# Tokens' rows scattered straight to their expert's part of a buffer, read back by plain loads; token ids stored 256 bytes apart

## The chip, the cores and the metric

The kernel runs on one core of one Trainium2 chip. The metric is the time of one execution on the device in microseconds (us). Before the change three executions took 4009.82, 4017.08 and 4010.77, with a median of 4010.77.

## What is computed

Three layers follow each other: a spectral filter over the sequence, a mixture of 8 experts in which each token goes to one, and a dense layer with a squared relu.

```python
# x (8, 3072, 256); filt_r, filt_i (1537, 256); moe_w1 (8, 256, 1024), moe_w2 (8, 1024, 256)
X = np.fft.rfft(x, axis=1)
y = np.fft.irfft(X * (filt_r + 1j * filt_i)[None], n=3072, axis=1)      # 24576 tokens of 256
logits = y @ w_gate;  e_idx = argmax(logits);  gate_w = softmax(logits)[e_idx]
eom = 1 / (1 + exp(-(y @ w_output_gate)))
for e in range(8):                                                    # MoE1: only the tokens of e
    out[mask] = gate_w * eom[:, e] * (relu(y[mask] @ w1[e]) @ w2[e])
h = relu(out @ moe2_w_in);  result = h * h @ moe2_w_out                  # MoE2: 256 -> 2048 -> 256
```

## The kernel before

The filter is done as matrix products in stages. Stage a loads x, stage b does the second half of the transform, the multiplication by the filter (in part on GpSimd, L340) and the first half of the inverse, stage c the last half. The eight batches are taken as four groups of two, and a group of stage c gives six chunks `yo` of 128 x 8 tokens. A row of a chunk has 272 floats (1088 bytes): 256 values, then logits and the scale of the token. `route` finds each token's expert and its rank there, with a running count per expert in `carry`. Products are made of operands split into a high and a low part of reduced precision (tiles with names in h and l), so each product is three matmuls, and the split costs ScalarE and VectorE a pass each.

Routing before: a chunk is stored to `yd` in token order (L471, 24 stores of 1088 KB). The slot that a token has among its expert's tokens is computed, and `scatter` (L405) writes the row number of each token, 4 bytes, to that slot of a table in DRAM, 128 tokens per indirect DMA on GpSimd, 192 in all. There are four tables, taken in turn, which twelve stores of zeros clear at the start; a reader adds the four.

MoE1 takes tiles of tokens of one expert. The first four (`KP`), of the expert with most tokens in the first three groups, are worked while stage c is still busy with the last group: this is called the lead stage here. After the last group `tables` computes on VectorE which expert, slot and output column each of the other 58 tiles has (37 wide ones of 512 tokens, 21 narrow ones of 256, two wide and one narrow in turn). For a tile `start_t` reads these three numbers into SP's registers (L714) and loads the tile's piece of the four tables (L719), `list_rows` adds them on VectorE, and `gather` (L739) fetches the rows from `yd` by 128 per indirect DMA on GpSimd, at step f = 4 of the tile two ahead. `load_w` loads 512 KB of weights per quarter tile on SP (L727, L728). `scale_x` and `turn_x` scale and transpose the rows (L765, L777, L782), `up` and `down` are the two products (L798, L814) with eight steps f each. At its end a tile stores its result to `ytd` (L822) and the row numbers of its tokens to `idsc` (L823). For a narrow tile row c x 128 + p lies on partition p, so that every piece of that store is 4 bytes; for a wide tile partition p has four tokens in a row, and a piece is 16 bytes.

During MoE1 the weights of MoE2 are decoded from 64-bit floats: `decode` loads a raw piece on SP (L612, 32 pieces of 256 KB) and works it on VectorE (from L617) between MoE1's own work. MoE2 loads 512 tokens of `ytd` and their ids, and scatters its result to the output's rows on GpSimd (L937, 192 in all).

Each engine works its instructions in program order. The order of the work between stages is a list of steps written out beforehand; in a step the generators named above issue their next piece. SP holds most DMAs, so a DMA there comes behind all that SP was given before; SP's DMAs take eight semaphores in turn, so one waits for the landing of the eighth before it. Buffers from pools make a writer wait for the last reader of the same buffer.

Of the kernel before, what the change touches and what calls it, by code (L numbers as in the profile page):

```python
# [11 lines left out]
F32 = mybir.dt.float32  # L12
# [17 lines left out]
SEG = NT  # L30
TP = E * SEG // 128 + 16
TT = 512
TC = 8
TS = 256

# [65 lines left out]
def spectral_moe_kernel(ctx: ExitStack, tc: tile.TileContext, x, filt_r, filt_i, w_gate, w_og, w1, w2,  # L101
# [6 lines left out]
    yd = dram.tile([NT + 1, YW], F32, name="yd")  # L108

    NTAB = 4  # L110
    ytd = dram.tile([D, NT + TT], F32, name="ytd")
    idsc = dram.tile([NT + TT, 1], I32, name="idsc")
    tab = [dram.tile([128 * TP, 1], I32, name=f"tab{i}") for i in range(NTAB)]
    tabv = [t.rearrange("(p c) o -> p (c o)", p=128) for t in tab]

# [9 lines left out]
    nc.gpsimd.iota(rowid, pattern=[[2 * S, PR], [1, N2]], base=1, channel_multiplier=N2)  # L125
# [31 lines left out]
    const.tile([128, 72], F32, name="pad")  # L157
    pl = {"xsm": ctx.enter_context(tc.tile_pool(name="xsm", bufs=2, side="right"))}
    right = lambda stack, name, bufs, **kw: stack.enter_context(tc.tile_pool(name=name, bufs=bufs, side="right", **kw))
    pl["xsm"].tile([128, 24], F32, name="xpad", bufs=1)  # L160
# [7 lines left out]
    zi = fcon.tile([128, E * SEG // 384], I32, name="zi")  # L168
    nc.gpsimd.memset(zi, 0)
# [88 lines left out]
    nc.scalar.dma_start(out=yd[0:1], in_=zrow)  # L258
# [103 lines left out]
    ydv = yd[1:NT + 1].rearrange("(p q j) d -> q p (j d)", p=PR, j=N2)  # L362
# [38 lines left out]
    def scatter(n):  # L401

        for _ in range(min(n, len(scat))):
            si, a, g, n = scat.pop(0)
            nc.gpsimd.indirect_dma_start(  # L405
                out=tab[nscat[0] % NTAB], out_offset=bass.IndirectOffsetOnAxis(ap=si[:, a:a + 1], axis=0),
                in_=rowid[:, g, n:n + 1], in_offset=None)
            nscat[0] += 1

    def route(c):  # L410
# [52 lines left out]
        sn, sq = (rp.tile([128, TC], I32, name=n, bufs=1) for n in ("sn", "sq"))  # L463
        nc.vector.tensor_copy(sn, sl)
        nc.vector.tensor_scalar(sq, sn, 7, None, op0=ALU.logical_shift_right)
        nc.vector.tensor_scalar(sn, sn, 127, None, op0=ALU.bitwise_and)
        nc.vector.scalar_tensor_tensor(si, sn, float(TP), sq, op0=ALU.mult, op1=ALU.add)
        if ncarry[0] == GP * UC // 4:
            nc.vector.tensor_tensor(cnt_p, c1, segb, ALU.subtract)
        yield  # L470
        later.append(lambda: nc.sync.dma_start(out=ydv[:, g, 2 * j0 * YW:(2 * j0 + TC) * YW],  # L471
                                               in_=t.rearrange("p j w -> p (j w)")))
        for a in range(TC):
            scat.append((si, a, g, 2 * j0 + a))
# [58 lines left out]
    def find_lead():  # L533
# [12 lines left out]
        v.tensor_scalar(leadi[:, 1:2], leadi[:, 1:2], 7, None, op0=ALU.logical_shift_right)  # L546

    def tables():
# [49 lines left out]
        v.tensor_scalar(tabi[:, 1:2], tabi[:, 1:2], 7, None, op0=ALU.logical_shift_right)  # L598
# [100 lines left out]
    W, WR, X, cols, ereg = {}, {}, {}, {}, {}  # L699
# [12 lines left out]
    def start_t(t):  # L712
        w = width[t]
        e, s, cols[t] = (nc.sync.value_load(tabi[slot[t - KP]:slot[t - KP] + 1, i:i + 1], min_val=0, max_val=m)  # L714
                         for i, m in enumerate((E - 1, (E * SEG - w) // 128, NT)))
        n = w // 128
        ti = pl["xsm"].tile([128, NTAB * 4], I32, name="ti", bufs=4)
        for i in range(NTAB):
            nc.sync.dma_start(out=ti[:, i * n:(i + 1) * n], in_=tabv[i][:, ds(s, n)])  # L719
        X[t] = ti  # L720
        ereg[t] = e
# [9 lines left out]
    def gather(t):  # L731
        n = width[t] // 128
        if t < KP:
            idx = idx_p[0][:, t * n:(t + 1) * n]
        else:
            idx = list_rows(X[t], n)
        xg = pl["xgq"].tile([128, 4 * YW + 2 * E], F32, name="xg", bufs=1)
        for c in range(n):
# [29 lines left out]
    def turn_x(t, h):  # L768
        xs, idx = X[t][:2]
        if h == 0:  # L770
            X[t] = xs, idx, *(pl["xgp"].tile([128, 2, TT], F32R, name=n) for n in ("xh", "xl"))
# [366 lines left out]
```

## Time and profile before

| | us |
|---|---|
| median of three executions | 4010.77 |
| profiled execution | 4012.15 |
| its span, first to last instruction | 4010.2 |
| TensorE busy in the span | 3841.1 (96%) |
| VectorE, ScalarE, GpSimd busy | 2836.9, 2000.6, 775.8 |
| mean granted clock of TensorE (share of full speed) | 0.982 |

The span runs from the filter (to about 720, with the lead stage from about 625), over MoE1 (to about 1970) to MoE2. The profile names an instruction by line, engine and operation, with out<-in by the program's tile names. "Idle before" is how long the engine had nothing to run, with what ended it: an instruction, a DMA that landed, or "remote", a semaphore event that no instruction in the trace explains. "PEclk" is the granted clock of TensorE. "SPq" rows are DMAs issued by SP; they are not busy time. A share of DMA is the mean over the core's 16 DMA engines, and may pass 1 where transfers are counted in a window that they only touch.

### The profile page before, as it was taken

The numbers are of one execution on the slowest core, as the hardware profiler recorded it, in microseconds if no ns is written. First come the engines' busy times: TensorE is split into PE (matmuls) and PEld (weight loads), VectorE is DVE, ScalarE is ACT, GpSimd is POOL, SyncE is SP. The second block draws the span as 40 slices with busy tenths as digits, with TensorE's granted clock in tenths as the row PEclk, the third lists the DMA queues.
The fourth block names the chain that finished last, engine by engine and source line by source line (L and its number), as shares of the span: only waits on it lengthen the run. The fifth ranks groups of instructions, "written<-read, shape, count | busy, mean of one in ns | idle before, by whom it ended". The sixth has DMA issues, their size and how long they took to land.

```text
span 4010.2 us, 75055 instructions
## 1 busy us (share of the span) xinstructions
PE 3841.1 (96%) x27556; PEld 3573.5 (89%) x27556; DVE 2836.9 (71%) x5265; ACT 2000.6 (50%) x3957; POOL 775.8 (19%) x743
## 2 busy tenths in 40 slices
PE   8988897898999999999999999999999999999998
PEld 7777775687788888888899999999999999999998
DVE  7576675477788886666677777777777777777775
ACT  6364553244445445455455555555555555555554
POOL 3354545311111111211001011010110100101001
PEclk9999998999999999999999999999999999999999
DMA  6323222155666666666300000000000000000000
GB/s 222 105 78 114 89 75 72 59 151 145 154 155 175 172 161 164 158 159 162 100 22 28 28 25 30 22 28 28 24 28 26 27 28 23 27 27 26 29 17 17
DMA packets 270773, 318.74 MB, mean 79 GB/s; under 512 B 82082, under 2 KB 215427, under 8 KB 267331
## 3 DMA queue, kind: packets, MB, share of 16 engines
q1 hardware_dynamic: 244128, 259.71, 23.6%
q0 software_dynamic: 25248, 53.99, 4.5%
q8 instruction: 216, 3.54, 0.4%
q14 instruction: 155, 1.26, 0.1%
q10 hardware_dynamic: 1026, 0.23, 0.0%
HBM read 231.55 MB, written 82.26 MB: 78 GB/s over the span
## 4 chain that ended last, share of the span: by engine, by line
PE 87%; DVE 4%; DMA 3%; another core or an unknown queue 2%; issue 2%; ACT 1%; SPq 0%; POOL 0%; DVEq 0%; POOLq 0%; ACTq 0%
PE py L928 26%; PE ph L882 17%; PE ph L798 12%; PE py L814 12%; PE px L882 7%; PE o L357 3%; PE p L378 2%; PE o L392 2%; PE p L278 2%; PE p L331 1%; PE p L335 1%; PE p L306 1%; PE px L777 1%; DMA raw<-in_moe_w_in_dram 1%
## 5 line engine op out<-in xcount | busy, mean ns | idle before, releaser
L928 PE MATMUL py<-woh,hh 128*128 128x256 f32 x3072 | 857.1, 279 | 0.0
L928 PE MATMUL py<-woh,hl 128*128 128x256 f32 x3072 | 852.8, 278 | 0.4 <-DVE hl L915 0.4
L928 PE MATMUL py<-wol,hh 128*128 128x256 f32 x3072 | 852.9, 278 | 0.0
L928 PEld LDWEIGHTS py<-woh,hl 128*128 128x128 f32 x3072 | 579.8, 189 | 0.9 <-DVE hl L915 0.8
L928 PEld LDWEIGHTS py<-woh,hh 128*128 128x128 f32 x3072 | 579.9, 189 | 0.0
L928 PEld LDWEIGHTS py<-wol,hh 128*128 128x128 f32 x3072 | 576.3, 188 | 0.0
L937 POOL DMA_INDIRECT out_dram<-ou,io x192 | 207.9, 1083 | 1868.6 <-ACT C L904 1634.6
L802 ACT ACTIVATE hh<-ph 128x512 fp32r<-128x512 f32 (+1 forms) x496 | 261.2, 527 | 596.9 <-PE ph L798 537.8
L882 PE MATMUL ph<-bh,wsh 128*128 128x256 f32 x1920 | 542.1, 282 | 5.1 <-ACT s L889 2.7
L882 PE MATMUL ph<-bl,wsh 128*128 128x256 f32 x1920 | 537.6, 280 | 0.1
L882 PE MATMUL ph<-bh,wsl 128*128 128x256 f32 x1920 | 537.3, 280 | 0.0
L906 DVE SCALAR_TENSOR_TENSOR q<-C 128x1024 f32<-128x1024 f32 x384 | 470.2, 1224 | 1.9 <-ACT C L904 1.9
L915 DVE TENSOR_TENSOR hl<-q,hh 128x1024 fp32r<-128x1024 f32 x384 | 467.1, 1216 | 1.1 <-ACT hh L913 1.1
L803 DVE SCALAR_TENSOR_TENSOR hl<-ph,hh 128x512 fp32r<-128x512 f32 (+1 forms) x496 | 296.4, 598 | 232.5 <-ACT hh L802 205.8
L900 DVE TENSOR_TENSOR C<-ph,p 128x256 f32<-128x256 f32 x384 | 163.1, 425 | 399.7 <-ACT hh L913 397.4
L913 ACT CAST hh<-q 128x1024 fp32r<-128x1024 f32 x384 | 403.9, 1052 | 1.3 <-DVE q L906 1.3
L904 ACT COPY C<-ph 128x256 f32<-128x256 f32 x384 | 144.1, 375 | 501.2 <-PE ph L882 501.2
L739 POOL DMA_INDIRECT xg<-yd,idx x190 | 199.4, 1050 | 948.9 <-DVE idx L749 902.0
L882 PEld LDWEIGHTS ph<-bh,wsh 128*128 128x128 f32 x1920 | 362.4, 189 | 8.3 <-ACT s L889 4.1
L814 PE MATMUL py<-hh,wh 128*128 128x512 f32 (+1 forms) x992 | 363.4, 366 | 0.0
L882 PEld LDWEIGHTS ph<-bl,wsh 128*128 128x128 f32 x1920 | 360.8, 188 | 0.3 <-DVE bl L860 0.3
L882 PEld LDWEIGHTS ph<-bh,wsl 128*128 128x128 f32 x1920 | 360.9, 188 | 0.0
(267 smaller groups left out, 8772.1 us busy)
## 6 DMA issues: line engine op xcount, KB each, us to landing
r<-in_moe_w_dram SPq DMA_DIRECT2D x472, 256.0 KB
yd<-yo SPq DMA_DIRECT2D x24, 1088.0 KB
xt<-in_x_dram SPq DMA_DIRECT2D x48, 512.0 KB
r<-ytd SPq DMA_DIRECT2D x48, 512.0 KB
ytd<-yt SPq DMA_DIRECT2D x41, 512.0 KB
ytd<-yt SPq DMA_DIRECT2D x21, 256.0 KB
raw<-in_moe_w_in_dram SPq DMA_DIRECT2D x16, 256.0 KB
raw<-in_moe_w_out_dram SPq DMA_DIRECT2D x16, 256.0 KB
```

Source lines behind the costliest of these rows:

```text
L739: nc.gpsimd.indirect_dma_start(out=xg[:, c * YW:(c + 1) * YW], out_offset=None, in_=yd[0:(NT * GP // NG if t < KP else NT) + 1], in_offset ...
L798: nc.tensor.matmul(ps, a[:, c, f2 * 128:(f2 + 1) * 128], b[:, c, 0:w], start=n == 0, stop=n == 5)
L802: nc.scalar.activation(hh, ps, AF.Relu)
L803: nc.vector.scalar_tensor_tensor(hl, ps, 0.0, hh.bitcast(F32), op0=ALU.max, op1=ALU.subtract)
L814: nc.tensor.matmul(Y[t][h], a[:, f % 2, h * 128:(h + 1) * 128], b, start=f == 0 and i == 0, stop=f == NF - 1 and i == 2)
L882: nc.tensor.matmul(ps, x[:, u, a], y[:, b], start=start and n == 0, stop=n == 2, skip_group_check=True)
L900: nc.vector.tensor_tensor(C[:, 3], V, p5, ALU.add)
L906: nc.vector.scalar_tensor_tensor(q, C, 0.0, C, op0=ALU.max, op1=ALU.mult)
L913: nc.scalar.copy(hh, q)
L915: nc.vector.tensor_tensor(hl, q, hh.bitcast(F32), ALU.subtract)
L928: nc.tensor.matmul(Z[t][k][:, c, :], x[:, 2 * i + k, c * 128:(c + 1) * 128], w[:, 2 * u + i, :], start=u == 0 and m in (0, 6), stop=u == N ...
L937: nc.gpsimd.indirect_dma_start(out=out, out_offset=bass.IndirectOffsetOnAxis(ap=io[:, c:c + 1], axis=0), in_=ou[:, c, :], in_offset=None)
```

## The change

Routing after: each chunk's rows go straight from the chunk to their slots in one DRAM buffer `srt`, in which every expert has room for all tokens and 256 more (`SEG`), by the same 192 indirect DMAs (L404), now with 1088 bytes per token. GpSimd writes the row number into a spare column of the chunk beforehand (L464). `yd`, its stores, the four tables, their clearing and loads, and `list_rows` are gone. `gather` is one plain load per tile on SP (L731) at f = 3. Behind each expert's last row 256 rows of zeros are stored by `tables` (L598, L599), at addresses read from the counts. The ids come with the rows: `scale_x` copies them (L752) and `put_ids` stores them one step later (L738), each 4 bytes to a row of 256 bytes in `idsc`, in one layout for all tiles. The scatters of chunks and of the output, and the lead tiles' gathers, are declared not to overlap, so that they don't wait for each other. In MoE2 the last unit's matmuls (L926, in `down2`) close half 0 of the output at m = 11 instead of 17.

```diff
-SEG = NT
-TP = E * SEG // 128 + 16
+SEG = NT + TS
...
+    srt = dram.tile([E * SEG, YW], F32, name="srt")
+    srtv = dram_disjoint_views(srt, NG * N2 + E)
+    outv = dram_disjoint_views(out, NT // 128)
...
+    idsc = dram.tile([NT + TT, 64], I32, name="idsc")
+    def apart(i, others, own):
+
+        tc.declare_no_dep(i.ins, group=others, reason="other rows")
+        tc.add_to_no_dep_group(own, i.ins)
...
     def scatter(n):
 
         for _ in range(min(n, len(scat))):
-            si, a, g, n = scat.pop(0)
-            nc.gpsimd.indirect_dma_start(
-                out=tab[nscat[0] % NTAB], out_offset=bass.IndirectOffsetOnAxis(ap=si[:, a:a + 1], axis=0),
-                in_=rowid[:, g, n:n + 1], in_offset=None)
+            t, si, a = scat.pop(0)
+            i = nc.gpsimd.indirect_dma_start(
+                out=srtv[nscat[0]], out_offset=bass.IndirectOffsetOnAxis(ap=si[:, a:a + 1], axis=0), in_=t[:, a], in_offset=None)
             nscat[0] += 1
+            if nscat[0] > GP * N2:
+                apart(i, "lead", "late")
...
-        sn, sq = (rp.tile([128, TC], I32, name=n, bufs=1) for n in ("sn", "sq"))
-        nc.vector.tensor_copy(sn, sl)
-        nc.vector.tensor_scalar(sq, sn, 7, None, op0=ALU.logical_shift_right)
-        nc.vector.tensor_scalar(sn, sn, 127, None, op0=ALU.bitwise_and)
-        nc.vector.scalar_tensor_tensor(si, sn, float(TP), sq, op0=ALU.mult, op1=ALU.add)
+        nc.vector.tensor_copy(si, sl)
+        nc.gpsimd.tensor_copy(t.bitcast(I32)[:, :, HD + 1], rowid[:, g, 2 * j0:2 * j0 + TC])
...
-        later.append(lambda: nc.sync.dma_start(out=ydv[:, g, 2 * j0 * YW:(2 * j0 + TC) * YW],
-                                               in_=t.rearrange("p j w -> p (j w)")))
...
+        endi = tile_("endi", dt=I32)
+        v.tensor_copy(endi, carry[ncarry[0] % 2][0:NTILE_T])
+        with tc.tile_pool(name="zp", bufs=1) as zp:
+            zero = zp.tile([128, 2 * YW], F32, name="zero")
+            nc.gpsimd.memset(zero, 0.0)
+            for e in range(E):
+                p = nc.sync.value_load(endi[0:1, e:e + 1], min_val=0, max_val=E * SEG - TS)
+                nc.sync.dma_start(out=srtv[NG * N2 + e][ds(p, TS)].rearrange("(p c) w -> p (c w)", c=2), in_=zero)
...
     def gather(t):
...
+        i = nc.sync.dma_start(out=xg[:, 0:n * YW].rearrange("p (c w) -> p c w", c=n),
+                              in_=srt[ds(srow.pop(t), w)].rearrange("(p c) w -> p c w" if w == TT else "(c p) w -> p c w", p=128))
         if t < KP:
...
+            apart(i, "late", "lead")
+        X[t] = xg
+
+    def put_ids(t):
+        nc.sync.dma_start(out=idsc[ds(cols[t], width[t]), 0:1].rearrange("(c p) o -> p (c o)", p=128), in_=IDS.pop(t))
...
-            nc.sync.dma_start(out=idsc[ds(c, w)].rearrange("(p c) o -> p (c o)" if w == TT else "(c p) o -> p (c o)", p=128), in_=idx)
...
-            i, k, c, n = m // 12, m // 6 % 2, m // 3 % 2, m % 3
+            k, i, c, n = m // 12, m // 6 % 2, m // 3 % 2, m % 3
...
-                    nc.gpsimd.indirect_dma_start(out=out, out_offset=bass.IndirectOffsetOnAxis(ap=io[:, c:c + 1], axis=0),
+                    nc.gpsimd.indirect_dma_start(out=outv[4 * t + c], out_offset=bass.IndirectOffsetOnAxis(ap=io[:, c:c + 1], axis=0),
...
-        if f == 4 and t + 2 < NTILE1 and t + 2 != KP:
+        if f == 3 and t + 2 < NTILE1 and t + 2 != KP:
             gather(t + 2)
```

GpSimd in the lead stage before: the indirect gathers of a lead tile (`xg`), four in a row, stand between the scatters (`tab`, of which eight or more come in a row) of the last group's chunks.

```order
L405 DMA tab_65<-rowid,si 198656x1
L405 DMA tab_66<-rowid,si 198656x1
L405 DMA tab_67<-rowid,si 198656x1
L405 DMA tab_68<-rowid,si 198656x1
L739 DMA xg<-yd,idxp 128x272 x4
L405 DMA tab_65<-rowid,si 198656x1
```

GpSimd in the same stage now, from the opening of the last group; `yo<-rowid` is the copy of the row numbers into a chunk.

```order
L404 DMA srt<-yo,si 198656x272 x14
L464 COPY yo<-rowid 128x8
L404 DMA srt<-yo,si 198656x272 x6
L464 COPY yo<-rowid 128x8
L404 DMA srt<-yo,si 198656x272 x8
L464 COPY yo<-rowid 128x8
L404 DMA srt<-yo,si 198656x272 x8
L464 COPY yo<-rowid 128x8
L404 DMA srt<-yo,si 198656x272 x8
L464 COPY yo<-rowid 128x8
L404 DMA srt<-yo,si 198656x272 x2
L464 COPY yo<-rowid 128x8
```

The gathers have left GpSimd; a copy stands ahead of the last scatters of the chunk before it.

SP where the tables are made, before: the raw load of the first decode follows the last chunk's store and a lead tile's result and ids, and the register loads from the table come behind it.

```order
L471 DMA yd<-yo 128x2176
L822 DMA ytd<-yt 128x2x512
L823 DMA idsc<-idxp 128x4
L612 DMA raw<-in_moe_w_in_dram 128x512
L714 TENSOR_LOAD tabi
L714 ISA x2
```

SP at the same place now, the last of the eight zero stores and what follows.

```order
L598 TENSOR_LOAD endi
L598 ISA x2
L599 ISA
L599 DMA srt<-zero 128x544
L811 DMA ytd<-yt 128x2x512
L613 DMA raw<-in_moe_w_in_dram 128x512
L738 DMA idsc<-ids 128x4x1
L715 TENSOR_LOAD tabi
```

The result's store and the raw load stand behind the register loads and the stores of zeros, which wait for the final counts.

SP in MoE1 before, from a tile's last table load to the ids.

```order
L719 DMA ti<-tab_68 128x4
L727 ISA
L727 DMA r<-in_moe_w_dram 128x2x256
L728 ISA
L728 DMA r<-in_moe_w_dram 128x2x256
L822 REGISTER_ALU
L822 DMA ytd<-yt 128x2x512
L823 REGISTER_ALU
L823 DMA idsc<-idx 128x4
```

SP in MoE1 now, from a tile's result to the next ids.

```order
L811 DMA ytd<-yt 128x2x512
L731 ISA
L731 DMA xg<-srt 128x2x272
L723 ISA
L723 DMA r<-in_moe_w_dram 128x2x256
L724 ISA
L724 DMA r<-in_moe_w_dram 128x2x256
L738 ISA
L738 DMA idsc<-ids 128x4x1
```

The gather of a tile two ahead stands in SP's queue between weight loads, and the ids are no longer stored with the result.

## Rows read from the trace of the kernel before

**Rows 1.** The page, busy time by engine

```profile
PE 3841.1 (96%) x27556; PEld 3573.5 (89%) x27556; DVE 2836.9 (71%) x5265; ACT 2000.6 (50%) x3957; POOL 775.8 (19%) x743
```

**Rows 2.** Windows by stage: length, then busy us of each engine, clock, DMA share, GB/s

```profile
960.00:1320.00 360.00, 339.22 (x1782) 289.86 (x1781) 281.88 (x620) 169.57 (x283) 59.09 (x57) 0.97 0.62 154
...
2025.00:3990.00 1965.00, 1961.97 (x16814) 1959.70 (x16813) 1460.51 (x2283) 1020.69 (x2143) 202.10 (x186) 1.00 0.08 26
```

**Rows 3.** Timeline of GpSimd, 676 to 711: start, duration, instruction, idle before

```profile
677.68 0.96 POOL L405 DMA_INDIRECT tab<-rowid,si  x1 [3.86 <-DMA tab<-rowid,si]
678.94 0.98 POOL L739 DMA_INDIRECT xg<-yd,idxp  x1 [0.30 <-issue]
...
708.63 0.96 POOL L405 DMA_INDIRECT tab<-rowid,si  x1 [0.31 <-issue]
```

**Rows 4.** Windows of three short stretches

```profile
676.00:713.00 37.00, 13.17 (x58) 9.42 (x57) 10.31 (x36) 5.50 (x14) 24.18 (x25) 0.65 0.24 73
...
270.00:288.00 18.00, 9.31 (x68) 8.65 (x68) 3.08 (x6) 3.53 (x8) 13.84 (x15) 0.90 0.13 37
...
962.00:968.00 6.00, 5.88 (x28) 4.55 (x26) 0.06 (x1) 2.68 (x5) 0.00 (x0) 1.00 0.70 32
```

**Rows 5.** Timeline of ScalarE, 680 to 714

```profile
694.86 0.59 ACT L781 CAST xh<-ph 128x512 fp32r<-128x512 f32 x1 [10.03 <-remote]
```

**Rows 6.** Timeline of TensorE: waits in the filter, the lead stage, MoE1; last matmul

```profile
290.17 1.28 PE L392 MATMUL o<-vt,m 128*128 128x272 f32 x2 [9.78 <-ACT yo L393]
...
712.93 1.27 PE L392 MATMUL o<-vt,m 128*128 128x272 f32 x2 [19.62 <-ACT yo L393]
...
974.84 1.11 PE L777 MATMUL px<-ident,xs 128*128 128x128 f32 x4 [6.96 <-DVE xl L782]
...
1101.92 0.69 PE L777 MATMUL px<-ident,xs 128*128 128x128 f32 x2 [7.55 <-DVE xl L782]
...
3994.45 0.28 PE L928 MATMUL py<-wol,hh 128*128 128x256 f32 x1
```

**Rows 7.** Timeline of SP's DMA issues, at the tables and in MoE1

```profile
786.87 0.58 SPq L612 DMA_DIRECT2D raw<-in_moe_w_in_dram  x1
792.13 9.50 SPq L719 DMA_DIRECT2D ti<-tab  x12
...
958.03 0.39 SPq L823 DMA_DIRECT2D idsc<-idx  x1
...
1369.43 0.36 SPq L823 DMA_DIRECT2D idsc<-idx  x1
...
1390.26 0.36 SPq L823 DMA_DIRECT2D idsc<-idx  x1
```

**Rows 8.** The chain in order of time: start, duration, what

```profile
958.52 13.50 DMA raw<-in_moe_w_in_dram
...
1102.60 2.56 PE py L814 x6
...
1107.48 1.39 PE py L814 x6
...
1109.58 1.39 PE py L814 x6
...
1115.07 5.59 DMA raw<-in_moe_w_in_dram
...
3994.91 2.41 DMA out_dram<-ou,io
```

**Rows 9.** Timeline of GpSimd, 3990 to the end

```profile
3994.91 0.96 POOL L937 DMA_INDIRECT out_dram<-ou,io  x1 [28.23 <-ACT ou L934]
...
4003.41 0.96 POOL L937 DMA_INDIRECT out_dram<-ou,io  x1 [1.71 <-DMA out_dram<-ou,io]
```

**Rows 10.** Timeline of VectorE, 788 to 796

```profile
793.15 0.28 DVE L617 TENSOR_SCALAR ea<-raw 128x256 int32<-128x256 int32 x1
```

**Rows 11.** Line L714: durations in ns (min/median/max), first and last start

```profile
L714 SPq TENSOR_LOAD <-tabi x174: 3/272/702, 790.2 to 1891.7; - x174
```

More of the change, by code (lines that the diff above doesn't have):

```diff
@@ L7 @@
 from concourse import mybir
+from concourse.ap import dram_disjoint_views
 from concourse.bass import ds
@@ L167, in spectral_moe_kernel @@
     mb2 = fcon.tile([128, 2, 96], F32, name="mb2")
-    zi = fcon.tile([128, E * SEG // 384], I32, name="zi")
-    nc.gpsimd.memset(zi, 0)
+    fcon.tile([128, 512], F32, name="zpad")
     zrow = fcon.tile([1, YW], F32, name="zrow")
@@ L713, in start_t @@
         w = width[t]
[L714 to L720, printed above, removed]
+        e, srow[t], cols[t] = (nc.sync.value_load(tabi[slot[t - KP]:slot[t - KP] + 1, i:i + 1], min_val=0, max_val=m)
+                         for i, m in enumerate((E - 1, E * SEG - w, NT)))
         ereg[t] = e
@@ L760, in scale_x @@
     def scale_x(t):
-        xg, idx = X[t]
+        xg = X[t]
+        n = width[t] // 128
+        IDS[t] = pl["xsm"].tile([128, 4], I32, name="ids", bufs=4)[:, 0:n]
+        nc.vector.tensor_copy(IDS[t], xg.bitcast(I32)[:, 0:n * YW].rearrange("p (c w) -> p c w", c=n)[:, :, HD + 1])
         xs = pl["xgp"].tile([128, 4, D], F32, name="xs", bufs=1)
@@ L765, in scale_x @@
             nc.vector.tensor_scalar(xs[:, c].rearrange("p (h w) -> p h w", h=2), v[:, :, 0:HD], v[:, 0, HD:HD + 1], None, op0=ALU.mult)
-        X[t] = xs, idx
+        X[t] = xs,
     def turn_x(t, h):
-        xs, idx = X[t][:2]
+        xs = X[t][0]
         if h == 0:
-            X[t] = xs, idx, *(pl["xgp"].tile([128, 2, TT], F32R, name=n) for n in ("xh", "xl"))
-        xh, xl = X[t][2:]
+            X[t] = xs, *(pl["xgp"].tile([128, 2, TT], F32R, name=n) for n in ("xh", "xl"))
+        xh, xl = X[t][1:]
         w = width[t]
@@ L846, in load_t @@
         nc.sync.dma_start(out=r, in_=ytd[:, t * TT:(t + 1) * TT].rearrange("(h p) t -> p h t", p=128))
-        ix = lpool[0].tile([128, 4], I32, name="ix")
-        nc.sync.dma_start(out=ix, in_=idsc[t * TT:(t + 1) * TT].rearrange("(p c) o -> p (c o)", c=4))
+        ix = lpool[0].tile([128, 4], I32, name="ix", bufs=4)
+        nc.sync.dma_start(out=ix, in_=idsc[t * TT:(t + 1) * TT, 0:1].rearrange("(c p) o -> p (c o)", p=128))
         R[t] = r, ix
@@ L860, in split_t @@
             nc.vector.tensor_tensor(blk(bl[:, i]), rv[j][k], blk(bh[:, i]).bitcast(F32), ALU.subtract)
-        io = lpool[0].tile([128, 4], I32, name="io")
-        nc.vector.tensor_scalar(io, ix, 1, None, op0=ALU.subtract)
-        X2[t] = bh, bl, io
+        X2[t] = bh, bl, ix
         yield
@@ L1035, in prelude @@
             yield
-        ti = pl["xsm"].tile([128, NTAB * 4 * KP], I32, name="tip", bufs=1)
-        n = 4 * KP
-        for i in range(NTAB):
-            nc.sync.dma_start(out=ti[:, i * n:(i + 1) * n], in_=tabv[i][:, ds(st, n)])
         load_w(0, 2)
@@ L1076, in spectral_moe_kernel @@
             next(fl[0], None)
-        if k == "b" and done["b"] < 3 * NTAB:
-            b = done["b"] % 3 * (E * SEG // 384)
-            nc.sync.dma_start(out=tabv[done["b"] // 3][:, b:b + E * SEG // 384], in_=zi)
         if k in gens:
```

62 lines of the change are left out of this document (20 added, 42 removed).

## The prediction

> **What bounds the kernel now.** I read the busy times first: TensorE is busy 3841.1 of 4010.2 us [rows 1], so only the idle 169 us, and stretches at a low clock, can move. The table by stages says where the idle time is. The last matrix stage (2025 to 3990) has 3 us of it in 1965, the middle of MoE1 (960 to 1320) 21 in 360 [rows 2]. So what the change takes from GpSimd or VectorE is worth time only where TensorE already waits. I went through TensorE's idle times one by one and kept those whose releaser is something that the change touches. There are three families, and a fourth place, where the change puts work ahead of a load that is soon needed.
>
> The first family lies where GpSimd issues many indirect DMAs back to back. One takes 0.96 us and the next follows 0.30 later, 1.26 together; from 677.68 to 708.63 there are 25 in a row, 8 of them gathers (L739) and 17 scatters (L405) [rows 3]. In that stretch TensorE is busy 13.2 of 37 us, at a mean granted clock of 0.65 [rows 4]. ScalarE's evictions there start late, with a releaser that the profile calls "remote", 10.03 us at 694.86 [rows 5], and TensorE then waits 19.62 us at 712.93 for such an eviction [rows 6]. Each later group of the inverse stage opens with 14 scatters in a row; the stretch 270 to 288 is one of three alike [rows 4], and behind it TensorE waits 9.78 us at 290.17 [rows 6]. The idle time of these stretches fits 1.26 x (n - 6) for n in a row: 10 for 14, 24 for 25. That is an estimate from those rows.
>
> The second is the store of the token ids of a narrow tile, 256 ids of 4 bytes side by side. One is issued at 958.03 [rows 7], half a microsecond ahead of a raw load for MoE2's weights, which lands 13.50 us after its issue, where one clear of such a store takes 5.59 [rows 8]. While it is in flight (962 to 968) the DMA engines are busy 0.70 but move 32 GB/s [rows 4], against 154 at 0.62 over the stage [rows 2]. VectorE, which works in order, stands at the decode for the load, and TensorE waits 6.96 us at 974.84. The twin at 1101.92 waits 7.55 [rows 6], after which TensorE runs at its lower clock: twelve matmuls take 4.88 us (1102.60 to 1107.48), the next twelve 2.10 [rows 8]. Behind the other 19 narrow stores no raw load is waited for so long.
>
> The third is the tail. The last matmul ends at 3994.7 [rows 6], but the four scatters of the output go one at a time from 3994.91 to 4003.41 [rows 9], each waiting until the one ahead has landed, 2.41 us [rows 8].
>
> **The change part by part.** The sum is made against the profiled execution, 4012.15 us with a span of 4010.2; the median of the three times is 1.4 below it.
>
> *Tail.* Each output scatter gets a view of its own, so none waits for another, and the last unit finishes half 0 six matmuls earlier. The first two go at about 3994.2 and 3995.5, the others at 3996.75 and 3998.0, 1.26 apart [rows 3]; the last issue moves from 4003.41 to 3998.0: **-5.4 us**. The waits that the other 188 lose lie beside a TensorE that is full [rows 2]. Bounds: -8 and -3.
>
> *Ids at a 256-byte pitch.* If it is lying side by side that makes the narrow store slow, both waits go, -(6.96 + 7.55) = -14.5, and the low clock behind each, 2 x (4.88 - 2.10) = 5.6: **-20 us**. For this: a wide store before writes 128 pieces, of 16 bytes, and loads behind it are not held; and the 192 scatters to the tables write 128 lots of 4 bytes each, far apart, every 1.26 us, without holding the DMA engines (0.24 busy at 73 GB/s [rows 4]). Against it: a wide store now has 512 pieces instead of 128. Bounds: -20, and the loss of rival D; I take the near end, since the scattered 4-byte writes are the nearest row.
>
> [...]
>
> *Gathers off GpSimd.* 206 gathers go, 198 us of GpSimd, most of them in MoE1 beside a busy TensorE: nothing there. What counts is the run of 25, which loses 8: 8 x 1.26 = 10.1 us less waiting, and less low clock in it, about the 2.8 above: **-13 us**. Bounds: 0 (the wait comes from something else) and -24 (the run breaks up, since GpSimd's new copies of the row numbers, which wait for evictions, now stand between every eight).
>
> *Scatters of rows instead of numbers.* The same 192, with 139 KB each instead of 512 bytes. On GpSimd a gather of 128 such rows takes 0.98, a scatter of numbers 0.96 [rows 3], so no change. The 24 stores of yd that they replace moved the same bytes. A chunk's buffer comes free when its eight scatters have landed, four chunks on: no wait. The new copies split an eight in six and two: **-1.5 us** over the inverse stage; bounds -12 (all three runs of 14 gain) and +10 (the copies hold scatters back, or row traffic delays evictions).
>
> *Zero stores ahead of the first decode.* After the counts are final, SP issues eight register loads and eight stores of 278 KB ahead of the raw load. Before, that load was issued at 786.87 [rows 7] and used at 793.15 with no wait [rows 10]. A DMA issue takes about 0.5; the 12 table loads from 792.13 with the 6 register loads between them took 9.50 [rows 7], so a register load takes 0.58. Eight of each with a 0.58 issue: 9.3, starting at 790.2, where SP's first register load from the table stands [rows 11], then the tile's store: raw goes out at about 800.5 and lands 5.6 later at 806, some 12 us after VectorE has come to it. Behind it on VectorE stand hl and xl subtractions, which TensorE needs within some 3 us: **+11 us**, 9 of waiting and 2 of low clock. Bounds: 0 (TensorE has enough left to do) and +20 (2.2 MB of zeros at 154 GB/s [rows 2], 14 us, land first).
>
> *The rest.* 232 table loads, 116 additions and three operations per route go; per tile a plain gather, a copy and a store of ids come, on engines with room. 12 zero fills of 256 KB go; nothing waited for them. 0, bounds -4 and +4.
>
> Sum: -5.4 - 20 - 13 - 1.5 + 11 = -29; 4012.15 - 29 = 3983, on the scale of the median 3982, and with the spare side of the run of 25 I say **3981**.
>
> **Rivals.** *B, the plus does not come.* If TensorE is not held behind the raw load, 11 more go: 3970; if the copies also break up the runs of 14, another 12: 3958. For it: what stands ahead of the raw load on VectorE may last longer than I read. Against: 12 us is several times what TensorE has in hand.
>
> *C, the runs of scatters hurt as before.* If the "remote" delays come from the traffic and not from the number of issues, -13 and -1.5 vanish: 3996. For it: the profile does not name what was late. Against: in 270 to 288 next to nothing moved, 37 GB/s, and it stalled all the same [rows 4].
>
> *D, slower: the 4-byte write itself is dear, not its neighbour.* A store of 256 held a load for 13.50 - 5.59 = 7.9 us more [rows 8]. A wide tile then has 512: 15.8. Stores of wide tiles are 20.83 us apart (1369.43 and 1390.26) [rows 7], of which the DMA engines are busy 0.62 x 20.83 = 12.9 [rows 2], so 7.9 are free. Once a wide store holds the engines longer than that, MoE1 is bound by DMA; at 15.8 it loses 7.9 on each of 37 wide tiles, 290: about 4270. For it: the narrow store is the only store of single ids in the trace, and it is slow. Against: the scatters.
>
> *E, slower: the gather comes late.* It now stands on SP behind weight loads of 256 KB, 1.7 us each at 154 GB/s [rows 2]. It is issued at f = 3, is needed about 13 us later in a narrow tile, and should land in 5 to 10, an estimate from the 5.59 of the raw load and four weight loads ahead. Where landing takes over 13 us it decides; late by 3 on each of 21 narrow tiles is +63 - 29: 4045.
>
> [...]
>
> **How the numbers follow.** The forecast 0.55, B 0.17, C 0.10, D 0.07, E 0.05; and 0.06 for pluses and minuses that cancel to within 0.2%, about what a measurement of this kernel can tell from no change (4003 to 4019). Faster: 0.55 + 0.17 + 0.10 = 0.82; slower 0.12. The likeliest case by itself spans 3970 to 3993. For 8 in 10 I add B and C: 3958 to 4003.
>
> **What would show it.** Tail: the four last scatters 1.3 us apart. Ids: the two raw loads landing in 4 to 6 us, no wait of TensorE for xl there. Bursts: TensorE's largest idle time in the lead stage near 10 us instead of 19.62. Tables: VectorE waiting about 12 us for the first raw load. It is wrong if the DMA engines are busy over 0.9 in MoE1 (D), if the scaling of a tile's rows waits for its gather (E), or if the lead stage keeps its 20 us (C).

## The result, and the profile after

The changed kernel took 3956.18 us (median of five runs, 3946.97 to 3958.95) against 4010.77 (five runs, 4005.17 to 4017.08): ratio 0.9857, 95% interval [0.9839, 0.9876], 54.6 us faster. The forecast was 3981 with a range of 3958 to 4003: the direction was right, the gain was nearly twice what was forecast, and the time lies just below the range. The profiled execution took 3946.97, the shortest of the five; so a comparison of the two profiles shows 65 us, of which the medians keep 55.

By the start times of the same instructions in both profiles (the count of a chunk, a lead or other tile's result copy, the last matmul) the 65 us split like this; differences are of unrounded times:

| stretch | from, to (before) | from, to (after) | difference | forecast |
|---|---|---|---|---|
| filter, to the last group's first count | 0, 659.8 | 0, 648.0 | -11.8 | -1.5 |
| lead stage, to the last count | 659.8, 759.5 | 648.0, 724.1 | -23.7 | -13 |
| tables and first tile behind them | 759.5, 857.8 | 724.1, 837.2 | +14.9 | +11 |
| rest of MoE1 | 857.8, 1964.5 | 837.2, 1913.6 | -30.4 | -20 |
| MoE2, to the last matmul | 1964.5, 3994.7 | 1913.6, 3934.7 | -9.1 | 0 |
| tail | 3994.7, 4010.2 | 3934.7, 3945.2 | -4.9 | -5.4 |

Busy times of the page after, to be read against [rows 1]; TensorE has the same matmuls, in a span 65 us shorter:

```profile
PE 3819.2 (97%) x27556; PEld 3560.0 (90%) x27556; DVE 2792.0 (71%) x5088; ACT 1998.8 (51%) x3957; POOL 575.2 (15%) x561
```

The middle of MoE1 after (window: length, busy us of PE, PEld, DVE, ACT, POOL, clock, DMA share, GB/s), against [rows 2]: 3.5 us idle in 360 instead of 21, at the full clock.

```profile
960.00:1320.00 360.00, 356.48 (x1940) 307.30 (x1939) 299.61 (x644) 184.06 (x309) 0.00 (x0) 1.00 0.54 170
```

GpSimd in the lead stage after (timeline), against [rows 3]. Between the eights stand the copies of row numbers; one of them, at 715.00, has waited 15 us for VectorE, and behind it sixteen scatters come in a row.

```profile
655.37 0.96 POOL L404 DMA_INDIRECT srt<-yo,si  x1 [0.30 <-issue]
656.33 1.24 POOL L464 COPY yo<-rowid 128x8 int32<-128x8 int32 x1
657.73 0.98 POOL L404 DMA_INDIRECT srt<-yo,si  x1 [0.16 <-issue]
...
715.00 0.20 POOL L464 COPY yo<-rowid 128x8 int32<-128x8 int32 x1 [15.24 <-DVE d L418]
715.75 0.98 POOL L404 DMA_INDIRECT srt<-yo,si  x1 [0.56 <-POOL yo L464]
```

TensorE's waits on ScalarE's yo, summed (us in total, times, longest), before:

```profile
PE o L392 <- ACT yo L393: 49.3, 12, 19.6
```

And TensorE's three largest sums after. The wait of 19.6 in the lead stage [rows 6] is gone; the longest now are two of the three behind the runs of 14, still there.

```profile
PE o L391 <- ACT yo L392: 33.3, 10, 10.5
PE o L391 <- DVE yo L392: 14.2, 8, 5.6
PE px L768 <- DVE xl L773: 13.4, 6, 7.0
```

At the tables, SP (start, duration of issue): the eight zero stores take 8.54 us, then the result of a tile, then the raw load at 771.83, which comes 15 us earlier than before [rows 7] in a kernel that was 35 us ahead by then.

```profile
762.49 8.54 SPq L599 DMA_DIRECT2D srt<-zero  x8
771.13 0.39 SPq L811 DMA_DIRECT2D ytd<-yt  x1
771.83 0.35 SPq L613 DMA_DIRECT2D raw<-in_moe_w_in_dram  x1
```

VectorE and TensorE behind it (two timelines), against [rows 10]: VectorE is held for 10.97 us (12 forecast), TensorE for 7.02 (9 forecast).

```profile
775.54 0.29 DVE L618 TENSOR_SCALAR ea<-raw 128x256 int32<-128x256 int32 x1 [10.97 <-DMA raw<-in_moe_w_in_dram]
```

```profile
778.07 1.11 PE L768 MATMUL px<-ident,xs 128*128 128x128 f32 x4 [7.02 <-DVE xl L773]
```

The tail (GpSimd's timeline), against [rows 9]: the four output scatters 1.27 apart, the last at 3938.00, as forecast.

```profile
3934.20 0.96 POOL L921 DMA_INDIRECT out_dram<-ou,ix  x1 [32.76 <-ACT ou L918]
...
3938.00 0.96 POOL L921 DMA_INDIRECT out_dram<-ou,ix  x1 [0.30 <-issue]
```

### The profile page after: what moved, and what is told of

Read it like the earlier page. It is cut to its first block, busy times and chain, and to the rows that moved or that the text cites. A ratio compares the mean times of both kernels' runs of the same rounds, so it can differ in the third digit from the quotient of the medians.

```text
span 3945.2 us, 74164 instructions
## 1 busy us (share of the span) xinstructions
PE 3819.2 (97%) x27556; PEld 3560.0 (90%) x27556; DVE 2792.0 (71%) x5088; ACT 1998.8 (51%) x3957; POOL 575.2 (15%) x561
## 4 chain that ended last, share of the span: by engine, by line
PE 72%; issue 14%; DVE 2%; POOL 2%; ACT 1%; another core or an unknown queue 0%; DMA 0%; SPq 0%; POOLq 0%; DVEq 0%; ACTq 0%
PE py L912 19%; PE ph L788 14%; PE py L804 14%; PE ph L866 12%; PE px L866 5%; PE o L391 2%; POOL out_dram L921 2%; PE p L377 2%; PE o L357 1%; PE px L768 1%; PE p L278 1%; PE p L331 1%; PE p L335 1%; PE p L306 1%
## 5 line engine op out<-in xcount | busy, mean ns | idle before, releaser
L921 POOL DMA_INDIRECT out_dram<-ou,ix x192 | 214.8, 1119 | 2987.9 <-ACT ou L918 2944.0
L788 PE MATMUL ph<-xh,wh 128*128 128x512 f32 (+1 forms) x992 | 353.7, 357 | 0.3 <-DVE hl L793 0.3
```

The lines of the kernel that those rows point to most:

```text
L788: nc.tensor.matmul(ps, a[:, c, f2 * 128:(f2 + 1) * 128], b[:, c, 0:w], start=n == 0, stop=n == 5)
L921: nc.gpsimd.indirect_dma_start(out=outv[4 * t + c], out_offset=bass.IndirectOffsetOnAxis(ap=io[:, c:c + 1], axis=0), in_=ou[:, c, :], in_o ...
```

## Experiments

All runs below are from later sets, in which the kernel before took 3899 to 3912 us and not 4011. Where no interval is given, a kernel ran once. What differs is told first, since every reading hangs on it. The waits for "remote" that stood behind runs of indirect DMAs are absent there. Summed waits of VectorE and ScalarE in the first profile of before:

```profile
DVE big L280 <- remote: 35.0, 8, 6.7
ACT big L280 <- remote: 26.5, 4, 6.7
ACT vt L381 <- remote: 23.7, 4, 9.5
DVE vt L381 <- remote: 22.9, 3, 10.0
```

In e3, before's scatters and gathers in the same order, no such line exists, and TensorE's waits for yo are these:

```profile
PE o L392 <- DVE yo L393: 3.8, 5, 1.8
```

The window 591 to 641 of e3, with runs of GpSimd's DMAs as long as in [rows 3], against the first of [rows 4]: 45 of 50 us busy at full clock, where before had 13 of 37 at 0.65.

```profile
591.00:641.00 50.00, 45.45 (x225) 34.87 (x226) 31.48 (x111) 16.92 (x43) 35.52 (x38) 1.00 0.41 146
```

None of the 18 later profiles has such a wait. Up to the last count of the filter before and e3 differ by 109 us (759.5 and 650.3), behind it by less than 10; from the first count to the last TensorE is idle for 100 us in before and for 22 in e3. In both first profiles every such wait of over 1 us lies beside or just behind a run of seven or more indirect DMAs, so some 100 of the 4011 us go with these waits, called stalls below. What holds the other engines there was not found. The later runs are recorded with their chips, which are three (9, 15 and 5); that of the first pair is not named, so whether the stalls belong to one chip stays open.

**e1, the pitch alone, in before.**

```diff
-    idsc = dram.tile([NT + TT, 1], I32, name="idsc")
+    idsc = dram.tile([NT + TT, 64], I32, name="idsc")
...
-            nc.sync.dma_start(out=idsc[ds(c, w)].rearrange(...), in_=idx)
+            nc.sync.dma_start(out=idsc[ds(c, w), 0:1].rearrange(...), in_=idx)
...
```

> The kernel before with one thing changed: idsc has 256 bytes per id, and every id store (at its old place, beside the tile's result and the raw load) writes 4 bytes at that pitch; a wide store now has 512 pieces instead of 128. Theory (lying side by side is what makes 256 four-byte pieces slow): the raw loads at about 958 and 1086 land in 4 to 6 us instead of 13.5, TensorE's waits of 6.96 and 7.55 us for xl go, and so do the smaller ones behind other narrow stores; MoE1 shortens by 25 to 30 us as it did in the changed kernel (tiles 8 to 36), in all 3980 to 3988. Rival 1 (in the changed kernel it was the place of the store, away from the raw load, that helped): the waits stay, 4005 to 4015. Rival 2 (the number of four-byte pieces counts): wide stores hold the engines too, 4100 or more.

3879.29 against 3906.08, ratio 0.9936 [0.9919, 0.9953]: 27 us from the pitch alone, the store at its old place. From the issue to the last of an id store's semaphore updates it takes 3.4 us (median of 62; longest 5.4), where narrow ones took 8.8 to 11.5 in e3, which has before's stores in the same set, and 9.2 to 11.3 in the first profile of before; no raw load takes over 6.1 (e3: up to 13.3). A wide store of 512 pieces is no slower than of 128: 3.8 us (median of 41; longest 5.6) in the first profile of the changed kernel, 3.7 (longest 5.4) in that of before. TensorE's waits for xl (us in total, times, longest), in e3 and then in e1:

```profile
PE px L777 <- DVE xl L782: 26.5, 13, 7.7
```

```profile
PE px L777 <- DVE xl L782: 9.1, 11, 2.0
```

The middle of MoE1, to be read beside [rows 2]:

```profile
960.00:1320.00 360.00, 355.34 (x1927) 305.19 (x1925) 301.60 (x654) 182.54 (x306) 67.34 (x63) 1.00 0.59 170
```

**e2, ids side by side again, in the changed kernel.**

```diff
-    idsc = dram.tile([NT + TT, 64], I32, name="idsc")
+    idsc = dram.tile([NT + TT, 1], I32, name="idsc")
```

> The changed kernel with the ids side by side again (4 bytes apart), 512 pieces per wide store and 256 per narrow one, at their new place one step after the scaling. Theory (side by side is slow): narrow stores hold the DMA engines some 8 us longer and wide ones some 16, against about 9 us that the engines have free per wide tile; loads of weights and raw pieces behind them land late in most tiles, MoE1 longer by at least the 30 us gained and up to 300: 3985 to 4260. Rival (the new place alone brought the gain): 3950 to 3962, as the changed kernel.

3924.30, ratio to before 1.0047 [1.0030, 1.0063], while the changed kernel in the next set has 0.9876: some 67 us lost. An id store now takes 10.1 us (median; wide and narrow alike). The same window again: DMA engines busier, fewer bytes, TensorE idle 26 us in 360.

```profile
960.00:1320.00 360.00, 334.40 (x1749) 283.17 (x1750) 269.49 (x585) 164.49 (x275) 0.00 (x0) 0.97 0.69 154
```

Together: the size of the piece is 4 bytes in all of these; 256 or 512 of them took 3.4 us at the pitch (e1) and 10.1 side by side (e2). Lying side by side is not dear by itself: the wide stores of before, 128 pieces of 16 bytes side by side, took 2.4 to 5.4 us. Whether the size or the number of the pieces makes that difference was not tried, nor a pitch between 4 and 256 bytes.

**e3, the layout of narrow tiles in MoE2, in before.**

```diff
-        by = "p (c q) -> p c q" if t < NWIDE else "p (q c) -> p c q"
+        by = "p (c q) -> p c q"
...
-        nc.sync.dma_start(out=ix, in_=idsc[...].rearrange("(p c) o -> p (c o)", c=4))
+        nc.sync.dma_start(out=ix, in_=idsc[...].rearrange("(p c) o -> p (c o)" if t < NWIDE else "(c p) o -> p (c o)", c=4))
```

> The kernel before with one thing changed: MoE2 reads a narrow tile's ids as (c p), so that its r is split in contiguous blocks instead of at a stride of 4 elements. Theory: the seven MoE2 tiles of narrow columns, each 42.63 us against 41.87 to 41.97 for the others, come down to the others' time, since their split copies on ScalarE and VectorE (0.67 and 0.61 us each) become 0.41; MoE2 is 5 us shorter, 4004 to 4008 in all. Rival (the output's views or the matmul order shorten these tiles): they stay at 42.63, 4008 to 4016.

3894.41 (one run). The last seven tiles take 41.87 us each instead of 42.63 (e1): together 293.1 against 298.5, -5.4 us. The groups of the last seven tiles in the first profile of before, by shape (busy us, mean ns): their r was read at a stride, 669 and 609 ns an operation.

```profile
L860 DVE TENSOR_TENSOR bl<-r,bh 128x256 fp32r<-128x256 f32 x21 | 11.6, 609 | 0.0
L859 ACT CAST bh<-r 128x256 fp32r<-128x256 f32 x19 | 11.5, 669 | 0.0
```

The same operations in the first profile of the changed kernel:

```profile
L846 DVE TENSOR_TENSOR bl<-r,bh 128x256 fp32r<-128x256 f32 x21 | 7.6, 421 | 0.0
L845 ACT CAST bh<-r 128x256 fp32r<-128x256 f32 x21 | 7.2, 409 | 0.0
```

The other 3.8 us of MoE2's 9.1 are 0.1 us in each of some 40 tiles, 41.97 or 41.87; both values occur in executions of either kind of kernel (before has both, e2 and e8 have 41.97, e12 41.87), so they are no part of the change.

**e4, one view of the output.**

```diff
...
-                    nc.gpsimd.indirect_dma_start(out=outv[4 * t + c], ...
+                    nc.gpsimd.indirect_dma_start(out=out, ...
```

> The changed kernel with the output scattered through the one tensor again, so that each output scatter waits for the landing of the one ahead. Theory (views matter at the tail alone): the end of the last matmul stays where it is in the changed kernel (3934.7 in its profile, up to the few us by which executions differ), and from there to the end it takes 4 to 6 us more (15 instead of 10.5). Rival (the views also save in MoE2, where 8 us were gained): MoE2 tiles take 41.97 or more instead of 41.87, another 5 to 8 us.

3859.15. From the last matmul to the end 15.22 us against 10.51 in e5; the tiles of MoE2 as in e5. The views are worth 4.7 us, all of it in the tail.

**e5, the changed kernel in a set without the stalls.**

> The changed kernel itself, once more, next to the one before. In the four runs so far GpSimd's runs of up to 25 indirect DMAs were as long as in the first profiles, but no eviction waited for a remote event, and the part up to the last route was about 100 us shorter in both kernels' relatives. Theory (the stalls behind runs of indirect DMAs belong to the chip or the execution, not to the kernel): where they are absent the change gains what they don't touch: ids 30, the end of the filter's groups 10, MoE2 8, tail 5, less 4 to 8 at the tables, in all 45 to 55 us or a ratio of 0.986 to 0.989. Rival (the stalls' relief in the lead stage is a large part of the gain everywhere): 25 to 40 us.

3856.28 against 3907.55, ratio 0.9876 [0.9859, 0.9893]: 51 us. Against e3's profile (which has the layout already): filter -11.7, lead stage -1.6, tables +7.2, rest of MoE1 -29.7, MoE2 +0.1, tail -4.9; with the layout's 5.4, and 1.5 lost ahead of the first count, -44.5, of the medians' 51 (e3's one time is some 6 us nearer to the changed kernel than its layout accounts for). So the lead stage's 24 us in the first profile were almost all relief of the stalls; the medians of the two sets gain nearly the same, 55 and 51, but not by the same parts. And 8 of the 15 us lost at the tables are not lost here; in the first profile TensorE waits 2.97 and 1.88 us behind the sixteen scatters in a row, which fits a stall but was not tried.

**e6, e9, e17, e18: the slot operations at a group's border.** The filter gains the same 12 us with and without stalls (11.8 and 11.7). TensorE's wait is at L331, for q from VectorE, at the border of each group. e6 puts three operations back behind the slot's conversion, e9 the old four ahead of it (the edit of e9):

```diff
...
+        nc.vector.tensor_copy(sn, sl)
+        nc.vector.tensor_scalar(sq, sn, 7, None, op0=ALU.logical_shift_right)
+        nc.vector.tensor_scalar(sn, sn, 127, None, op0=ALU.bitwise_and)
+        nc.vector.scalar_tensor_tensor(sx, sn, 197.0, sq, op0=ALU.mult, op1=ALU.add)
         nc.vector.tensor_copy(si, sl)
```

> The changed kernel with three small VectorE operations per chunk put back behind the slot's conversion (a shift, a mask and a multiply-add of 128 x 8 numbers, results unused). Theory (these three stood on TensorE's path at the border of each group, where VectorE routes the last chunk while TensorE waits for its first product q): TensorE's wait at L331 is 3.1 to 3.3 us again at the three borders, and each group's first route comes 2 to 3.5 us later, 7 to 10 in all by the last group. Rival (the 10 us came from the stores of yd or from scatters): no change against the changed kernel, 0 to 2 us.

> The changed kernel with the four slot operations of before in their old order on VectorE (convert, shift, mask in place, multiply-add), results unused, ahead of the conversion that is used. Theory (the multiply-add with its two inputs is held by GpSimd's multiplication at L340 whenever it starts while that one runs; at the three group borders it then takes 1.24 us instead of 0.17, as before the change, which e6 missed by starting 0.3 us ahead of it): the multiply-add takes 1.2 us at the borders, TensorE's wait at L331 there is about 3 us, the last group's first route comes 8 to 10 us later than in e5. Rival (length of the chain alone): 0.17 each, as e6, 2 to 3 us later.

e6: 3858.21, the last group's first count 2.7 us later than in e5; e9: 3858.84 and 3.2 later, wait at L331 1.93 instead of 1.24 (1.73 in e6). That is a third of what is missing, and both theories missed: what came is e9's rival, the length of the chain. In e3 the fourth operation took 1.24 and 1.26 us at the first and the last border (VectorE's timeline; 0.17 elsewhere):

```profile
191.03 1.24 DVE L467 SCALAR_TENSOR_TENSOR si<-sn,sq 128x8 int32<-128x8 int32 x1 [0.23 <-DVE sn L466]
```

GpSimd's timeline of e3 there: its multiplication of 1.26 us began 0.04 ahead of it and ended with it.

```profile
190.99 1.26 POOL L340 TENSOR_TENSOR q<-q,fb 128x512 f32<-128x512 f32 x1 [0.97 <-POOL q L340]
```

In e9 VectorE's operation started at 191.87, without the wait of 0.23 that it has in e3, and GpSimd's at 192.04: just ahead, and it took 0.17. So e17 adds two small operations ahead of it, and e18 has in its place one with a single input:

```diff
+        for _ in range(2):
+            nc.vector.tensor_scalar(sn, sn, 127, None, op0=ALU.bitwise_and)
         nc.vector.scalar_tensor_tensor(sx, sn, 197.0, sq, op0=ALU.mult, op1=ALU.add)      # e18: tensor_scalar(sx, sn, 197.0, 1.0, ...)
```

> e9 with two more one-input operations ahead of the multiply-add (two SBUF inputs, result unused), so that it starts 0.3 to 0.4 us later, inside GpSimd's multiplication at the three group borders instead of just ahead of it. Theory (it then waits for GpSimd's operation to end): it takes 0.9 to 1.2 us there instead of 0.17, TensorE's wait at L331 is 3.1 to 3.5 us instead of 1.93, the first route of the last group comes 4 to 6 us later than in e9. Rival (the 1.24 us have nothing to do with GpSimd): 0.17, and the waits grow by the 0.4 us only.

> e17 with the multiply-add replaced by an operation of the same size with one SBUF input and two constants. Theory: it is not held by GpSimd, 0.17 us, TensorE's wait at L331 2.3 us, the last group's first route 1 to 2 us later than in e9. Rival (any VectorE operation there is held while GpSimd works): as e17.

3866.81 and 3868.03. VectorE in e17 (timeline), with GpSimd's multiplication from 191.93 to 193.19 beside it: the second of the added operations is held until that ends (1.44 us for the two).

```profile
191.78 1.44 DVE L468 TENSOR_SCALAR sn<-sn 128x8 int32<-128x8 int32 x2
193.25 0.17 DVE L469 SCALAR_TENSOR_TENSOR sx<-sn,sq 128x8 int32<-128x8 int32 x1
```

TensorE there, of e17, then of e5: 3.41 against 1.24 us, and behind the longer wait the same two matmuls take 2.04 instead of 1.10: the granted clock is 0.50 there (195.5 to 199.8), against 1.00 in e5 (193.9 to 198.3).

```profile
195.49 2.04 PE L331 MATMUL p<-bi,mb 96*128 96x512 f32 x2 [3.41 <-DVE q L348]
```

```profile
193.91 1.10 PE L331 MATMUL p<-bi,mb 96*128 96x512 f32 x2 [1.24 <-DVE q L348]
```

The last group's first count comes at 581.4 in e17 and 581.7 in e18, 569.4 in e5, 579.6 in e3: the whole gain at the borders is given back, where the old chain without the hold gave back 3 us (e9). The collision is the cause. An operation with two inputs is not needed for it: it was one with one input that was held, in both, at all three borders (1.23 to 1.25 us), so e18 did not tell what it was made for. The operations held took 1.23 to 1.26 us against 0.17; what it is that they wait for in GpSimd's multiplication was not shown. Not every operation beside it was held: L339, whose p lies in PSUM, took 0.68 to 0.69 us where it started inside such a multiplication and 0.68 to 0.70 elsewhere (first profiles of both kernels).

One such collision is left in the changed kernel. At each border L459, further ahead in the same chain, takes 1.24 us instead of 0.17; VectorE and GpSimd in e5 (two timelines):

```profile
190.34 1.24 DVE L459 SCALAR_TENSOR_TENSOR s<-en,s 128x8 f32<-128x8 f32 x1
```

```profile
190.28 1.27 POOL L340 TENSOR_TENSOR q<-q,fb 128x512 f32<-128x512 f32 x1 [0.39 <-PE p L306]
```

What it costs was not tried.

**e7 and e16, the raw load ahead of the zeros.**

```diff
...
     tables()
     open_left()
     dec.append(decode_all())
+    next(dec[0])
+    zeros()                      # the eight register loads and stores, taken out of tables()
```

> The changed kernel with the first decode's raw load issued ahead of the eight register loads and stores of zeros. Theory (VectorE's wait for the raw load cost 7 us of TensorE and some low clock): VectorE doesn't wait for raw near the tables, TensorE's wait of about 7 us for xl there goes, from the second lead tile to the fourth 8 to 9 us less, ratio 0.002 below that of the changed kernel in the same call. Rival (the gather behind the zero stores, or the register loads for three tiles, is late next): the wait moves to a later tile and at most 3 us are gained.

> The raw load ahead of the zeros, once more, on what may be another chip. Theory: 5 to 8 us below the changed kernel (e13) whatever the stalls do, TensorE's 7 us wait for xl near the tables gone. Rival (where stalls end the lead stage, the tables are reached later and the load lands in time anyway): no difference.

3850.51 (ratio to before 0.9860 [0.9843, 0.9876]) and 3852.00 (0.9868 [0.9852, 0.9884]), 5.8 and 6.2 us below the changed kernel in the same sets (e5 3856.28, e13 3858.20). The raw load goes out at 652.59, VectorE does not wait for it, and TensorE's longest wait for xl falls from 6.9 (e5) to 1.1:

```profile
PE px L774 <- DVE xl L779: 4.8, 10, 1.1
```

By the third lead tile it is 8.4 us ahead of e5, at MoE1's end 5.3: 3 us are lost again over the rest of MoE1. The decode is a step ahead there; that this is the reason was not shown. This is the fastest version that was run; the intervals of its ratio and of the changed kernel's overlap.

**e8 and e12, the leftover scatters in stage b.**

```diff
                 v = u - g * UB
+                scatter(1)
```

e8 has the early raw load and, for the last chunk, the copy on VectorE besides.

> The changed kernel with three edits: the raw load ahead of the zeros, the scatters that are left over at a group's end issued one per step of the next group's stage b instead of 14 in a row at stage c, and the last chunk's row numbers copied on VectorE so that GpSimd's last 16 scatters don't all wait for that copy. Theory: 8 us from the raw load everywhere; where runs of indirect DMAs stall the other engines, another 25 to 35 (three runs of 14 cost 10 each, the last run of 16 about 5). Rival (stall is by number of scatters, not by their coming in a row): only the 8 us.

> The changed kernel with the 14 scatters that are left over at a group's end issued one per step of the next group's stage b. The combined kernel was 14.6 us slower than the changed one where nothing stalls, its groups 6 us longer each. Theory (GpSimd's multiplications of stage b stand behind these scatters, and TensorE behind them): 5 to 6 us later per group, 16 to 18 in all; where runs of 14 stall, 10 us per group are gained against it. Rival (the copy on VectorE or the early raw load did it): no loss here.

3870.91, ratio 0.9909 [0.9892, 0.9925], and 3871.61. e8 was expected to gain 8 us and lost 14.6 against e5. In e12 each group is 6 to 8 us later and the last one's first count 20.5, the loss that its theory had at 16 to 18. GpSimd's timeline of e12: a scatter ahead of every multiplication, no idle time left in the stage where TensorE waits for the product.

```profile
203.51 1.29 POOL L340 TENSOR_TENSOR q<-q,fb 128x512 f32<-128x512 f32 x1
204.97 1.28 POOL L404 DMA_INDIRECT srt<-yo,si  x1 [0.17 <-issue]
206.27 1.28 POOL L340 TENSOR_TENSOR q<-q,fb 128x512 f32<-128x512 f32 x1
```

**e10, e11, e13 to e15, aimed at the stalls.** Row numbers copied on VectorE (e10, e14), a memset behind each scatter of the second and third group's chunks (e11, e15), and the changed kernel as their control (e13).

> The changed kernel with the 24 copies of row numbers on VectorE instead of GpSimd, so that nothing but the slots' numbers paces GpSimd's scatters: up to 17 and more in a row in the lead stage. Theory (a run of indirect DMAs delays what other engines wait for, by 1.26 us for each beyond six; the copies, which wait for evictions, break the runs): where the execution shows such stalls at all, TensorE's waits in the lead stage are 10 to 20 us again; where it shows none (as in the second set of runs), no change beyond 2 us. Rival (the gathers on GpSimd were what stalled): no wait over 3 us in the lead stage.

> The changed kernel with a memset of 128 x 512 on GpSimd behind each scatter of the second and third group's chunks, so that scatters come 1.8 us apart instead of 1.26; the run of 14 ahead of the second group stays as it is. Theory (rate): where runs stall, the wait of 10 us behind the first run of 14 stays, and those behind the second and third run fall below 4 us. Rival (a scatter's number): they stay at 10. Where nothing stalls, no gain.

> The changed kernel a third time, as the control for the two below. Where evictions wait for remote events behind runs of scatters: three waits of 10 us behind the runs of 14 and next to none in the lead stage, as in its first profile; where not: as e5.

> Row numbers copied on VectorE, once more. Theory (long runs of scatters stall the other engines where such stalls are seen at all, and the copies on GpSimd break the runs): a wait of TensorE of 10 us or more in the lead stage that e13 doesn't have. Rival (the gathers in the run were the cause): none over 3 us there. Without such stalls: as e10.

> Scatters of the second and third group's chunks 1.8 us apart, once more. Theory (rate): the wait behind the first run of 14 stays at 10 us, those behind the second and third fall below 4. Rival (number): all three stay at 10. Without such stalls: as e11, 3861.

3859.99 and 3858.35, 3861.15 and 3860.67, 3858.20: none of them met the stalls, and without them none differs by more than 3 us from the changed kernel in the last of these sets (3858.20), or by more than 5 from e5. What breaks a stall, a shorter run, a lower rate or the copies, was not shown.

## Why the forecast was too high

*Right, with its size:* the tail, -5.4 forecast, -4.9 measured, and by e4 due to the views alone. The zero stores ahead of the decode: 9.3 us of SP forecast and 9.3 measured (761.7 to 771.0), 12 of VectorE's wait against 10.97; the raw load landed in 3.6 us and not 5.6. In the set without stalls the cost was +7.2.

*Right mechanism, too small:* the ids, -20 forecast. e1 shows -27 for the pitch alone, e5 -29.7 with the gather. The sum counted the two large waits with their low clock (0.54 from 1102.60 to 1107.48 before), 20.1, and put the other narrow stores at nothing ("no raw load is waited for so long"); by the times between one tile's result store and the next, the few tiles around those two waits gained 25 in the first pair (23.5 from e3 to e1), and what is left lies at later tiles (the largest 3.3 us, and 2.5 from e3 to e1).

*The step that failed* is "the rest: 0". Its "three operations per route" were put at nothing, as work that nothing waits for; at three places, the borders of the groups, TensorE waited for VectorE behind them. There one of the three was held 1.1 us by GpSimd. With the longer chain this cost TensorE 1.8 to 1.9 us of waiting each (3.13 against 1.24 at the first) and 1.7 to 3.2 at the low clock behind it: the five groups of matmuls behind each wait took 5.63, 6.92 and 7.14 us at a granted clock of 0.70, 0.56 and 0.54 (from 209.12, 384.21 and 561.25), and 3.97 at 1.00 after (from 208.01, 378.92 and 552.70). That is 13 us in all; the filter is 11.8 shorter, and e17 gives 12 back. And the change of layout was not in the sum at all: 5.4 us (e3). Both stood in the profile of before: the two operations' mean of 609 and 669 ns beside 419 and 408 in earlier tiles, and the hold with TensorE's wait behind it (VectorE's and TensorE's timelines):

```profile
205.89 1.23 DVE L467 SCALAR_TENSOR_TENSOR si<-sn,sq 128x8 int32<-128x8 int32 x1 [0.24 <-DVE sn L466]
```

```profile
209.12 1.82 PE L331 MATMUL p<-bi,mb 96*128 96x512 f32 x2 [3.13 <-DVE q L348]
```

*The lead stage*, -13 forecast, -23.7 in the first pair and -1.6 without stalls. The sum took a stall behind a run as a property of the kernel, and fitted it to one execution; the bound of -24 was met there. That anything came of this term is luck: it hangs on the set in which the pair was measured. Where nothing stalls, taking eight gathers out of a run of 25 was worth next to nothing (-1.6 in the lead stage), as rival C had it, though for another reason: not the traffic but the absence of the stall. The waits behind the runs of 14 stayed in the first pair (10.49, 10.50 and 5.64 us after; 9.78, 10.49 and 8.01 before), about as the forecast had them.

*Rivals.* B did not come, though the time is near its 3958: TensorE was held behind the raw load, and the runs of 14 kept their waits. D (every 4-byte piece is dear) is refuted by e1, E (a late gather) by the changed profile, where no scaling waits for its load. None of the forecast's signs of being wrong appeared (the DMA engines were busy 0.54 in MoE1): they were the signs of its rivals, and a cost put at nothing had none.

Worked again from what was measured in the first pair of profiles: -4.9 - 30.4 - 23.7 - 11.8 + 14.9 - 5.3 (layout) - 3.8 (0.1 us a tile in MoE2) = -65.0. This is the table of the result once more, so that it adds up shows nothing; the causes are shown one by one in e1, e3, e4 and e17, and that of the lead stage's -23.7 is open.

## What to carry to other kernels

Where an engine's idle time is named with another engine's instruction, look at how long that instruction and the few ahead of it take there, compared with the same lines elsewhere: here a 0.17 us operation took 1.23 at three places, and the filter without it and its chain was 11.8 us shorter. Store small pieces apart in DRAM when something waits behind them (27 us in e1), and put what is needed first ahead of a row of register loads (6 us in e7 and e16). A stall with no releaser in the trace should be seen in a second set of runs before a sum rests on it.

## What was not expected of the hardware

Id stores of 4-byte pieces took 3.4 us at 256 bytes apart (e1) and 10.1 side by side (e2), whether 256 or 512 pieces. A 0.17 us VectorE operation took 1.24 and 1.26 us where a GpSimd multiplication had started 0.04 and 0.03 us earlier (e3, first and last border). And beside the same runs of indirect DMAs evictions came up to 10 us late in the first two profiles and not at all late in the 18 later ones; the kernel before took 4011 us with it and about 3906 without.
